# One integer addition of a bitwise weight conversion changes its engine, and a stretch of MLP work changes its place in the issue order

## The chip, the cores and the metric

The kernel runs on one core of a Trainium2 chip. Its time is the device time of one execution in microseconds; before the change it is 1355.24 us, the median of five runs (1354.21 to 1356.5). A profile of one execution goes with it. The engines that matter here are TensorE (PE, matrix products, with its weight loads shown as PEld), VectorE (DVE), ScalarE (ACT), GpSimd (POOL) and SyncE (SP, which here only issues transfers). Each engine works through its own instructions strictly in the order in which the program issues them, and waits for the others through semaphores; so the place of an instruction in its engine's order is as much a part of the kernel as the instruction itself.

## The reference, cut to what matters

```python
# q, k, v: 8 batches x 8 heads x 576 rows x 64; w_in 512 x 2048; w_out 2048 x 512
scores = scale * q @ k.T
thresh = max(scores, -1) - tau
scores = where(scores >= thresh, scores, -1e9)
attn = exp(scores - max) ; attn /= sum(attn) + 1e-9
x = (attn @ v)              # heads side by side: 4608 tokens x 512
h = x @ w_in
out = (0.5 * h * (1 + erf(h / sqrt(2)))) @ w_out
```

The weights w_in and w_out come as 64-bit floats. The chip has no arithmetic for them, so the kernel reads their two 32-bit halves and puts a 32-bit float together with shifts, masks and an integer addition.

## The kernel before, in words

**Slots.** The attention is cut into slots. A slot is one pair of heads and one chunk of 128 query rows (i = 0 to 3) or the 64 rows left over of both heads (i = 4). Slots 0 to 7 are chunks 0 and 1 of the first batch's four pairs, slots 8 to 19 their chunks 2, 3 and 4; from slot 20 on one pair after the other is taken with all five chunks. `BATCH` is 20, so n = 20 is the first slot of the second batch. Slots 0 to 19 are called early here; they turn matrices with TensorE (L339, L309), later slots with VectorE and transfers.

**A slot's instructions.** `scores` gives TensorE the product q k (L393) into one or two tiles of PSUM. The tag has two buffers, so the scores of slot n+1 can be written only when slot n has done with its own. `softmax_head` then issues, for each tile, the maximum of a row (L405, VectorE), the threshold (L406, GpSimd: a 128x1 instruction) and the exponential (L408, ScalarE). `softmax_tail` later issues the masking with the sum (L424, VectorE), which reads the scores, the threshold and the exponential, and frees the scores' buffer; in early slots GpSimd adds 1e-9 to the sum (L427), and VectorE inverts it in the next slot (L433). `weigh_v` multiplies with v (L527), and `divide_early` multiplies the result by the inverse on GpSimd (L454, 128x256).

**The weight conversion.** The weights are cut into 32 pieces of 128x512: 16 of w_in, then 16 of w_out. `load_piece` fetches a piece raw, both halves (L183, issued by GpSimd after the first four). The generator `conversions` issues for each piece: two ScalarE instructions, one that brings the high half to a power (L201, into a tile `power`) and one that writes the low half's bits straight into the weight tile (L202); then three on VectorE: a shift and mask (L209), an and/or with the sign (L211), and the integer addition of `power` to the low bits in the weight tile (L214). After L214 the next raw piece is fetched, and `converted[0]` counts the piece. Each VectorE step yields a nominal price (340, 720, 640). `convert` is a planner with a debt: it is given so many nanoseconds in each slot and takes steps until the debt is paid. In an early slot from the fourth on it is called twice: for at least one step (or 700 in chunk 4) ahead of `softmax_tail`, and at the end of the slot with 3100 (2000 in slots 1 and 2, without limit from slot 19 on).

**The MLP.** `fill` issues the work of the MLP block by block: 64 products of the first layer (L603), then 32 of the second (L618). How much is due in a slot comes from a curve of goals; the difference to the slot before is added to `owed`. A product is issued only if enough pieces are counted in `converted`. In early slots `fill` runs after the scores of the slot, later at the end of the slot. The first layer's results are held until slot 20, when ScalarE loads the Gelu table, runs Gelu on all of them (`gelus_held`, L576) and loads the Exp table again (L589). So the second layer of block 0 begins at the end of slot 20.

Of the kernel before, what the change touches and what calls it, by code (L numbers as in the profile page):

```python
# [9 lines left out]
U32 = mybir.dt.uint32  # L10
U8 = mybir.dt.uint8
AF = mybir.ActivationFunctionType
ALU = mybir.AluOpType
# [5 lines left out]
def kernel(  # L19
# [28 lines left out]
    nc = tc.nc  # L48
# [46 lines left out]
    op = late_end.enter_context(tc.tile_pool(name="op", bufs=2))  # L95
# [50 lines left out]
    for _ in range(3):  # L146
# [4 lines left out]
    pieces = [(w_in_sb[c][:, f:f + PIECE], moe_w_in[c * P:(c + 1) * P, f:f + PIECE])  # L151
              for f in range(0, d_ff, PIECE) for c in range(N_DM)]
# [3 lines left out]
    LATER = 2  # L156
    raws = []
    loaded = [0]
    converted = [0]
# [26 lines left out]
    def conversions():  # L186

        vec = nc.vector
        ahead = []
        while raws or ahead:
            if raws:
                dst, raw, slot = raws.pop(0)
                lo, hi = (raw.rearrange("p (f w) -> p f w", w=2)[:, :, i] for i in range(2))
                power = gp.tile([P, PIECE], U32, tag="g", name="power")  # L200
                nc.scalar.activation(power.bitcast(FP32), hi.bitcast(FP32), AF.Copy, bias=0.0, scale=2.0 ** -112)  # L201
                nc.scalar.activation(dst.bitcast(U32), lo, AF.Copy, bias=0.0, scale=2.0 ** -29)  # L202
                ahead.append((dst, hi, power, slot))
                yield 0
            if len(ahead) == LATER and converted[0] == len(pieces) - LATER:
                yield None
            if len(ahead) == 2 or not raws:
                dst, hi, power, slot = ahead.pop(0)
                vec.tensor_scalar(power, power, 3, 0x7FFFFFF8, op0=ALU.logical_shift_left, op1=ALU.bitwise_and)  # L209
                yield 340  # L210
                vec.scalar_tensor_tensor(power, hi, 0x80000000, power, op0=ALU.bitwise_and, op1=ALU.bitwise_or)  # L211
                x_free.extend(slot)
                yield 720
                vec.tensor_tensor(dst.bitcast(U32), power, dst.bitcast(U32), op=ALU.add)  # L214
                load_piece()
                converted[0] += 1
                yield 640

    conv = {"steps": None, "debt": 0.0}

    def convert(ns, least=0):

        if conv["steps"] is None:
            conv["steps"] = conversions()
        conv["debt"] += ns
        while conv["debt"] > 0 or least > 0:
            took = next(conv["steps"], None)
            if took is None:
                return
            conv["debt"] -= took  # L230
            least -= took
# [164 lines left out]
    def softmax_head(p, i):  # L396

        s = st[p]
        n = len(s["sc", i])
        nmx = small.tile([P, 2], FP32, tag="nmx", name="nmx")  # L400
        thr = s["thr", i] = small.tile([P, 2], FP32, tag="thr", name="thr")
        w = s["p", i] = work.tile([P, 2 * S], FP32, tag="p", name="p")
        for e in range(n):
            sc = s["sc", i][e][:, :, 0:HALF]
            nc.vector.tensor_reduce(nmx[:, e:e + 1], sc, axis=AXIS.XY, op=ALU.max, negate=True)  # L405
            nc.gpsimd.tensor_scalar(  # L406
                thr[:, e:e + 1], nmx[:, e:e + 1], -1.0, tau_eff, op0=ALU.mult, op1=ALU.subtract)
            nc.scalar.activation(  # L408
                w[:, e * S:(e + 1) * S].rearrange("p (h s) -> p h s", h=2), sc, AF.Exp, bias=nmx[:, e:e + 1], scale=1.0)
# [20 lines left out]
    def invert(p, i):  # L430

        den = st[p]["sum", i]
        nc.vector.reciprocal(den, den)  # L433
# [193 lines left out]
    def fill(ns, tokens):  # L627

        mlp["debt"] += ns
        while True:  # L630
            if mlp["next"] is None:
                n = mlp["n"]
                if n == PLAIN or (n + 1) * TOK > tokens:
                    break
                mlp["steps"] = block_steps(n)
                mlp["n"] += 1
                mlp["next"] = next(mlp["steps"])
            took, need = mlp["next"]
            if mlp["debt"] <= 0 or need > converted[0]:
                break  # L640
            mlp["debt"] -= took
            mlp["next"] = next(mlp["steps"], None)
# [22 lines left out]
    vec, pool = nc.vector, nc.gpsimd  # L665
# [15 lines left out]
    def weights_first():  # L681
        room = tail["room"] = early_end.enter_context(tc.tile_pool(name="wsum", bufs=1, side="right", reuse_waits="tile"))
        tail["s"] = room.tile([P, 4, 2, 2, P], FP32, name="s_out")
        tail["ss"] = room.tile([P, 4, 3, P], FP32, name="s_in")
        tail["sp"] = room.tile([P, 3, 4, P], FP32, name="s_plain")
        tail["t"] = room.tile([P, 4, 2, HD], FP32, name="t_out")
        w_in_sums(vec, 0)
# [338 lines left out]
    BATCH = HP * SLOTS  # L1026
# [18 lines left out]
    tokens = 0  # L1045
    owed = 0.0
# [3 lines left out]
    for n in range(len(slots) + WEIGH + 1):  # L1050
        p, i = slots[n] if n < len(slots) else divmod(n, SLOTS)
        early = p < EARLY
        last = slots[n - 1] if 0 < n <= len(slots) else None
        if p < NP:
            scores(p, i)
            softmax_head(p, i)
            if last and last[0] < EARLY:
                invert(*last)
            if p < HP - 1 and i == 0:
                turn_qk_early(p + 1)  # L1060
        elif n == len(slots):
            early_end.close()
            weights_first()
        gelus(0)
        if n == BATCH:
            gelus_held()
        table()
        for args in due:
            weigh_v(*args)
            divide_early(*args)  # L1070
        due = []
        if p > EARLY and i == WEIGH:
            for lo, hi in (0, WIDE), (WIDE, S):
                weigh_v(p - 1, lo, hi)
            if p == NP:
                divide(p - 1)
        owed += (goal(n) - goal(n - 1)) * BLK_NS * (PARTS[i] if not early and p < NP else 1.0)
        if early:
            fill(owed, tokens)
            owed = 0.0  # L1080
            table()
        if last and last[0] < EARLY and last[1] < NC:
            turn_p_early(*last)
        if early and n > 2:
            convert(0, 700 if i == NC else 1)
        if p < NP:
            softmax_tail(p, i)
        if p < NP and not early:
            turn_p(p, i)
        if p < NP and not early:  # L1090
            if i == 2:
                regroup(p, 1)
            if i > 2:
                regroup(p, i)
            if i == NC:
                divisors(p)
        if last and last[0] < EARLY and last[1] == NC:
            turn_p_early(*last)
        if p < 2 and i == 0:
            for _ in range(2):  # L1100
                load_piece()
            load_v_early(p + 2)
        if p == 1 and i == NC:
            load(HP)
        if n == BATCH - 3:
            load(HP + 1)
        if n == BATCH:
            for t in pd_tail + [turned_p[:, e, h, :, :] for e in range(2) for h in range(2)]:
                nc.gpsimd.memset(t[:, NB:4 * KR, :], 0.0)
        if EARLY < p < NP and i == DIVIDE:  # L1110
            divide(p - 1)
        if p >= HP and i == 1 and p + 2 < NP:
            loads = load_steps(p + 2)
        if p >= HP:
            next(loads, None)
        if p >= HP and i == 1 and p + 1 < NP or p == HP - 1 and i == 2:
            scale_q(p + 1)
        if p >= HP - 1 and i == 2 and p + 1 < NP:
            turn_qk(p + 1)
        convert(0 if n == 0 else 2000 if n < 3 else 3100 if n < BATCH - 1 else 1e9)  # L1120
        if not early:
            lag[0] = 2 if p < NP else 0
            fill(owed, tokens)
            owed = 0.0
        if last and last[0] < EARLY:
            if last[1] == 1:
                due.append((last[0], 0, TOK))
            if last[1] == NC:
                due.append((last[0], TOK, S))
        if n == START - 1:  # L1130
            tokens = TOK
        elif n == BATCH + 1:
            tokens = S
        elif p > EARLY and i == DIVIDE and p % HP == 0 or p == NP and i == WEIGH:
            tokens = p // HP * S
            leaving += [n for n in AWAY if n in x_blk and (n + 1) * TOK <= tokens]
        elif leaving and i < 2:
            put_away(leaving.pop(0))
# [35 lines left out]
```

## Time and profile before

| | value |
|---|---|
| median of five runs | 1355.24 us |
| the profiled execution itself | 1356.08 us, of it 1354.3 us span |
| slots 1 to 19, from the first L405 of slot 1 to that of slot 20 | 13.40 to 138.29 us |
| L209 shift and mask, VectorE | 32 of 419 ns (median) |
| L211 and/or, VectorE | 32 of 691 ns (median) |
| L214 integer addition, VectorE (shown as a custom instruction on 128x1024 uint16) | 32 of 692 ns (median) |
| VectorE busy over the span | 1056.8 us (78%) |
| GpSimd busy over the span | 623.5 us (46%) |
| largest idle of GpSimd | 366.8 us, ahead of L406, for the maximum L405 |

The page of a profile gives busy time by engine, forty equal slices of the span, and groups of instructions; the trace behind it can be asked for a table of stretches, for the instructions of one engine in order of time, or for one line. A row of the last kind reads: start, duration, engine, line, operation, output <- inputs, shape, number, and in brackets the idle time before it with what ended it. Where a duration includes waiting for a shared resource, the row is longer than its fellows. The start of one instruction to the start of the next (the pitch) can be shorter than the duration, since the recorded ends overlap a little.

A slot starts, for this document, with its first L405 in the VectorE rows: slot 2 at 19.57 us, slot 10 at 71.49, slot 16 at 110.85, slot 17 at 116.03, slot 18 at 125.88, slot 19 at 134.70, slot 20 at 138.29, slot 21 at 150.13, slot 22 at 159.19.

### The profile page before, as it was taken

Reading aid. Unit: us, or ns where it says so; the run is one execution under the profiler, and the core shown is the slowest. Engines: PE = TensorE matmul, PEld = TensorE weight load, DVE = VectorE, ACT = ScalarE, POOL = GpSimd, SP = SyncE. Lnnn points to the kernel's source line nnn. Section 1 sums busy time; section 2 is a strip of 40 time slices with the busy share of each in tenths; the row PEclk is TensorE's granted clock in tenths of the full one; section 3 lists DMA queues with packets and bytes.
Section 4 is the critical chain, followed back from the end, with each engine's and each line's share of the span. In section 5 each row is a group of like instructions: output and inputs, shape, how many; then the busy total and the mean of one; then the engine's idle time right before and its main releaser. Section 6 shows DMA issues by size and latency. Waiting matters only on the chain.

```text
span 1354.3 us, 19808 instructions
## 1 busy us (share of the span) xinstructions
PE 1323.9 (98%) x6282; PEld 892.5 (66%) x6282; DVE 1056.8 (78%) x2029; ACT 605.6 (45%) x1027; POOL 623.5 (46%) x1065
## 2 busy tenths in 40 slices
PE   8799899999999999999999999999999999999998
PEld 6476457467457457557557557568787787877877
DVE  6987677788888888878888888875758598385775
ACT  7786527547547538527637636413201112211120
POOL 5442354555555554554555552145363513625530
PEclk9799899999999999999999999999999999999999
DMA  8642277677778787787688777500000041000003
GB/s 271 178 158 50 58 158 162 142 162 185 155 178 184 161 192 179 161 206 170 152 202 188 151 174 157 120 9 1 0 1 0 8 117 32 1 1 0 1 0 78
DMA packets 209782, 152.40 MB, mean 113 GB/s; under 512 B 113360, under 2 KB 193088, under 8 KB 209680
## 3 DMA queue, kind: packets, MB, share of 16 engines
q1 hardware_dynamic: 188224, 112.53, 37.5%
q0 software_dynamic: 21024, 38.32, 9.9%
q8 instruction: 51, 0.84, 0.3%
q14 instruction: 51, 0.42, 0.1%
q10 hardware_dynamic: 432, 0.30, 0.1%
HBM read 55.97 MB, written 12.52 MB: 51 GB/s over the span
## 4 chain that ended last, share of the span: by engine, by line
PE 88%; DMA 1%; ACT 1%; DVE 1%; issue 0%; SPq 0%; POOL 0%; DVEq 0%; ACTq 0%; POOLq 0%
PE bank L791 34%; PE o_ps L618 17%; PE hT L603 15%; PE sc L393 12%; PE xT L527 10%; DMA x<-xall 1%; ACT p L408 0%; DVE nmx L405 0%; PE tr L339 0%; DVE p L424 0%; ACT L576 0%; SPq L476 0%; SPq L474 0%; ACT g L570 0%; ACT xall L537 0%
## 5 line engine op out<-in xcount | busy, mean ns | idle before, releaser
L408 ACT ACTIVATE p<-sc,nmx 128x576 f32<-128x576 f32 x288 | 201.9, 738 | 287.1 <-DVE nmx L405 286.9
L424 DVE SCALAR_TENSOR_TENSOR p<-sc,thr,p 128x576 f32<-128x576 f32 x288 | 225.2, 815 | 66.7 <-ACT p L408 64.1
L406 POOL TENSOR_SCALAR thr<-nmx,tau_eff 128x1 f32<-128x1 f32 x288 | 89.7, 312 | 383.3 <-DVE nmx L405 366.8
L603 PE MATMUL hT<-xall,w_in 128*128 128x256 f32 x1024 | 242.8, 386 | 2.6 <-ACT g L570 2.6
L405 DVE TENSOR_REDUCE nmx<-sc 128x1 f32<-128x576 f32 x288 | 205.3, 750 | 51.1 <-PE sc L393 50.0
L618 PE MATMUL o_ps<-w_out,g 128*128 128x512 f32 x512 | 239.4, 608 | 3.7 <-ACT g L576 3.7
L603 PEld LDWEIGHTS hT<-xall,w_in 128*128 128x128 f32 x1024 | 189.6, 190 | 53.1 <-issue 23.0
L673 DVE TENSOR_TENSOR c<-c,bank 128x320 f32<-128x320 f32 x304 | 147.2, 487 | 33.7 <-PE bank L791 20.1
L673 DVE TENSOR_TENSOR o<-o,bank 128x256 f32<-128x256 f32 x240 | 99.6, 419 | 93.8 <-PE bank L791 88.8
L618 PEld LDWEIGHTS o_ps<-w_out,g 128*128 128x128 f32 x512 | 94.0, 192 | 114.4 <-issue 107.8
L393 PE MATMUL sc<-kT,qT 64*128 64x288 f32 x960 | 162.2, 434 | 7.0 <-DVE p L424 6.3
L527 PE MATMUL xT<-pT,v 128*64 128x256 f32 (+1 forms) x1280 | 167.2, 415 | 0.1
L488 DVE STREAM_TRANSPOSE turned_p<-p 128x1152 f32<-128x1152 f32 x112 | 154.4, 1379 | 3.9
L393 PEld LDWEIGHTS sc<-kT,qT 64*128 64x128 f32 x960 | 92.5, 188 | 81.5 <-issue 68.0
L527 PEld LDWEIGHTS xT<-pT,v 128*64 128x64 f32 x1280 | 90.5, 140 | 75.5 <-issue 17.4
L791 PE MATMUL bank<-w_out,c 128*128 128x256 f32 x480 | 120.2, 381 | 0.5 <-DVE o L673 0.5
L259 POOL DMA_DIRECT2D v<-in_v_dram x208 | 110.9, 536 | 4.0 <-issue 1.8
L791 PEld LDWEIGHTS bank<-w_out,c 128*128 128x128 f32 x480 | 89.9, 190 | 18.8 <-DVE o L673 3.0
L844 ACT ACTIVATE c<-c 128x320 f32<-128x320 f32 (+1 forms) x80 | 46.9, 624 | 114.6 <-DVE c L673 114.5
L791 PE MATMUL bank<-t_out,c 128*128 128x256 f32 x320 | 82.8, 381 | 0.0
L791 PE MATMUL bank<-t_out,g 128*128 128x256 f32 x320 | 82.1, 379 | 0.0
L673 POOL TENSOR_TENSOR c<-c,g 128x320 f32<-128x320 f32 (+1 forms) x40 | 50.5, 1271 | 67.5 <-DVE c L673 67.5
(179 smaller groups left out, 1743.8 us busy)
## 6 DMA issues: line engine op xcount, KB each, us to landing
pT<-turned_p SPq DMA_DIRECT2D x448, 160.0 KB, 3.6
pT<-pd_tail SPq DMA_DIRECT2D x112, 80.0 KB, 3.0
q<-in_q_dram POOLq DMA_DIRECT2D x104, 72.0 KB, 3.7
k<-in_k_dram POOLq DMA_DIRECT2D x104, 72.0 KB, 3.2
inv<-turned SPq DMA_DIRECT2D x54, 128.0 KB, 4.1
v<-in_v_dram POOLq DMA_DIRECT2D x156, 40.0 KB, 3.1
out_dram<-o SPq DMA_DIRECT2D x40, 128.0 KB, 2.4
xall<-in_moe_w_out_dram POOLq DMA_DIRECT2D x9, 512.0 KB, 4.0
```

The source lines that it names most:

```text
L259: eng.dma_start(t[r:P:4, e, 0:n, :], rows[:, r * KR:r * KR + n, :])
L393: nc.tensor.matmul(sc[e][:, h, 0:HALF], lhsT=lhsT, rhs=s["kT"][rows, at:at + HALF], start=True, stop=True)
L405: nc.vector.tensor_reduce(nmx[:, e:e + 1], sc, axis=AXIS.XY, op=ALU.max, negate=True)
L406: nc.gpsimd.tensor_scalar(thr[:, e:e + 1], nmx[:, e:e + 1], -1.0, tau_eff, op0=ALU.mult, op1=ALU.subtract)
L408: nc.scalar.activation(w[:, e * S:(e + 1) * S].rearrange("p (h s) -> p h s", h=2), sc, AF.Exp, bias=nmx[:, e:e + 1], scale=1.0)
L424: nc.vector.scalar_tensor_tensor(row, sc[e][:, :, 0:HALF], thr[:, e:e + 1], row, op0=ALU.is_ge, op1=ALU.mult, accum_out=den[e])
L488: nc.vector.transpose(turned_p[:, :, i // 2, 0:NB, i % 2 * Q:(i % 2 + 1) * Q], w.rearrange("p (e b i) -> p e b i", e=2, i=Q))
L527: nc.tensor.matmul(to, lhsT=s["v"][:, e, c, :], rhs=rhs, start=(c == 0), stop=(c == KR - 1))
L603: nc.tensor.matmul(hT[:, j % 2, :], lhsT=w_in_sb[c][:, j * P:(j + 1) * P], rhs=x_blk[n][:, c, :], start=(c == 0), stop=(c == N_DM - 1))
L618: nc.tensor.matmul(o[:, 0:d_model], lhsT=g[j][:, m * P:(m + 1) * P], rhs=w_out_sb[j], start=(j == 0), stop=(j == N_DF - 1))
L673: eng.tensor_tensor(out, a, b, op=ALU.add)
L791: nc.tensor.matmul(to, lhsT=l, rhs=r, start=start and k == 0, stop=k == len(pairs) - 1, skip_group_check=not start)
```

## The change

```diff
         ahead = []
+        done = 0
         while raws or ahead:
...
-            if len(ahead) == LATER and converted[0] == len(pieces) - LATER:
+            if len(ahead) == LATER and done == len(pieces) - LATER:
                 yield None
...
                 x_free.extend(slot)
                 yield 720
-                vec.tensor_tensor(dst.bitcast(U32), power, dst.bitcast(U32), op=ALU.add)
+                sums_due.append((dst.bitcast(U32), power))
                 load_piece()
-                converted[0] += 1
-                yield 640
+                done += 1
+                yield 0
+
+    sums_due = []
+
+    def add_low_bits():
+
+        while sums_due:
+            dst, power = sums_due.pop(0)
+            nc.gpsimd.tensor_tensor(dst, power, dst, op=ALU.add)
+            converted[0] += 1
...
             scores(p, i)
             softmax_head(p, i)
+            add_low_bits()
...
-        convert(0 if n == 0 else 2000 if n < 3 else 3100 if n < BATCH - 1 else 1e9)
+        convert(0 if n == 0 else 1200 if n < 3 else 2200 if n < BATCH - 1 else 1e9)
         if not early:
             lag[0] = 2 if p < NP else 0
-            fill(owed, tokens)
-            owed = 0.0
+            if n != BATCH:
+                fill(owed, tokens)
+                owed = 0.0
```

The third VectorE instruction of each piece is no longer issued. Its operands are put on a list, and the additions on the list are issued to GpSimd in the next slot, behind that slot's thresholds; only then is the piece counted. The next raw piece is fetched without the addition being waited for. A piece now costs 1060 in the planner's money, and a slot's budget falls from 3100 to 2200 (2000 to 1200 in slots 1 and 2). In slot 20 `fill` isn't called; what was due there stays in `owed` and is issued at the end of slot 21, behind the scores of slot 21.

## The prediction

> **What bounds the kernel now.** I read the page first, for the engine that is full, then the slots one by one.
>
> ```profile
> PE 1323.9 (98%) x6282; PEld 892.5 (66%) x6282; DVE 1056.8 (78%) x2029; ACT 605.6 (45%) x1027; POOL 623.5 (46%) x1065
> ...
> PE   8799899999999999999999999999999999999998
> ...
> DVE  6987677788888888878888888875758598385775
> ...
> PEclk9799899999999999999999999999999999999999
> ```
>
> TensorE is full from the sixth slice (170 us) on; only the first five have gaps, and there its clock falls too. The change touches only those slices. Since TensorE is full after them, a microsecond won or lost before 160 us should reach the end whole. The table of stretches, cut at the slots (here 6, 7, 12, 17, 18, 20), shows who is full there:
>
> ```profile
> core 0: us, PE busy (x) PEld busy (x) DVE busy (x) ACT busy (x) POOL busy (x), PEclk, DMA share, GB/s
> ...
> 44.62:51.04 6.42, 3.73 (x12) 2.34 (x14) 6.21 (x14) 4.77 (x9) 2.46 (x6) 0.67 0.52 158
> 51.04:58.32 7.28, 7.13 (x52) 4.67 (x48) 5.62 (x14) 5.09 (x11) 2.91 (x6) 0.82 0.48 143
> ...
> 82.99:91.30 8.31, 8.02 (x53) 6.50 (x50) 6.04 (x14) 5.56 (x13) 3.70 (x7) 1.00 0.42 151
> ...
> 116.03:125.88 9.85, 9.85 (x65) 7.01 (x63) 8.06 (x18) 5.89 (x12) 1.29 (x4) 1.00 0.12 30
> 125.88:134.70 8.82, 6.20 (x25) 5.00 (x25) 6.32 (x13) 5.07 (x11) 2.60 (x5) 0.81 0.01 3
> ...
> 138.29:150.13 11.84, 8.09 (x26) 3.72 (x27) 5.53 (x12) 8.91 (x14) 1.34 (x8) 0.86 0.01 1
> ```
>
> The column after the length is TensorE, the third VectorE, the fifth GpSimd. Slot 6 is VectorE's: 6.21 of 6.42 us. Slots 7 and 12, with a product with v, aren't: there L209 waits for ScalarE's L201 (1.59 and 2.20 us idle), and ScalarE for TensorE. GpSimd has room: 2.5 to 3.7 us a slot.
>
> **What the removal is worth.** In slot 6 the conversion's starts on VectorE stand like this:
>
> ```profile
> 47.82 0.69 DVE L211 SCALAR_TENSOR_TENSOR power<-xall,power 128x512 uint32<-128x512 uint32 x1
> 48.54 0.69 DVE L214 CUSTOM_DVE_ANT_0 w_in<-power,w_in 128x1024 uint16<-128x1024 uint16 x1
> 49.15 0.42 DVE L209 TENSOR_SCALAR power<-power 128x512 uint32<-128x512 uint32 x1
> ```
>
> From start to start L211 costs 0.72 to 0.73 us, L214 0.61, and L209 0.45: 1.79 a piece before, 1.18 after. The 32 pieces save 32 x 0.61 = 19.5 us of VectorE, if nothing takes its place. I follow the planner's debt by hand: 3100/1700 = 1.82 pieces a slot before, 2200/1060 = 2.08 after. So slots 3 to 15 hold 24 L209, 23 L211 and 24 L214 before (42.2 us) and 27, 27 and none after (31.9 us): 10.3 us less. The conversion also ends earlier: slot 18 has its last two pieces before, slot 17 after; slot 18 then holds none.
>
> **What the addition costs on GpSimd.** No row shows an integer addition there. The nearest are float additions and subtractions of the same shape, and L454:
>
> ```profile
> L673 POOL TENSOR_TENSOR s_out<-w_in 128x512 f32<-128x512 f32 x6 | 7.6, 1266 | 0.0
> ...
> L454 POOL TENSOR_TENSOR xall<-xall,inv 128x256 f32<-128x256 f32 x8 | 6.8, 848 | 13.8 <-ACT inv L448 13.8
> ```
>
> I take 1.27 us, the row of the same shape and operation. Bounds: 0.69 us, as on VectorE, and 2.5 us, twice the row. The Trainium skill speaks against the move: "GPSIMD Engine Reference", section 4.1, keeps elementwise work on VectorE, and section 3.1 gives 4497 ns for 2048 floats, by which I estimate 1.12 us for 512; the sum below would then be about 1.4 us lower (nine blocks of 0.15 us). The float rows here say 1.27.
>
> The cost isn't GpSimd's time but what it takes from VectorE. In slot 5, L211 meets an L454:
>
> ```profile
> 40.21 0.81 DVE L424 SCALAR_TENSOR_TENSOR p<-sc,thr,p 128x576 f32<-128x576 f32 x1
> ...
> 40.95 1.05 DVE L211 SCALAR_TENSOR_TENSOR power<-xall,power 128x512 uint32<-128x512 uint32 x1
> ```
>
> ```profile
> 39.03 0.45 POOL L406 TENSOR_SCALAR thr<-nmx,tau_eff 128x1 f32<-128x1 f32 x1 [0.27 <-DVE den L433]
> 40.71 0.75 POOL L454 TENSOR_TENSOR xall<-xall,inv 128x256 f32<-128x256 f32 x1 [1.22 <-ACT inv L448]
> ```
>
> L211 takes 1.05 us instead of 0.69 and ends 0.6 after L454 does: it stood still while GpSimd ran. The other stretched L211 (1.20 and 1.11 us, at 129.43 and 106.86) stand beside an L454 as well. In the other direction L406, 0.29 us alone, takes 0.45 to 0.72 beside an L209 or L211. L424 isn't touched (0.81 us beside GpSimd's L551 at 195 us).
>
> So in a full slot that starts at T: second threshold done at about T+2.0, first addition to T+3.3, under the two L424 (to T+3.3): free. The second runs to T+4.6 and meets the L209 and L211 after L424, which wait: about 1.2 us. If VectorE gets in first, the addition gets in at the next gap, and the price is the same. **Sum, slots 3 to 15:**
> - Slots bound by VectorE (3, 4, 5, 6, 8, 10, 11, 13, 14): instructions +0.24 - 0.77 - 1.22 x 6 - 0.77 = -8.6 us; blocks 1.2 in seven of them, 2.4 in slot 13 (three additions), none in slot 3 (one): +10.8 us. Net +2.2.
> - Slots 7, 9, 12, 15 wait for ScalarE; the removed L214 stood in that wait, so nothing is won. In 9 and 12 one L211 or L209 more follows the wait: +0.6 and +0.5.
> - Slots 1 and 2: one L214 less ahead of L405 of slot 2: -0.6. Slot 3 starts when TensorE's scores are there: 0.
>
> Together +2.7 us, by bounds from -8.1 (no block) to +14 (an addition of 2.5 us blocks once for 2.5).
>
> **Slots 16 to 19.** Here TensorE shows what VectorE delays:
>
> ```profile
> 128.60 1.94 PE L603 MATMUL hT<-xall,w_in 128*128 128x256 f32 x4 [2.62 <-ACT g L570]
> ...
> 142.95 5.98 PE L618 MATMUL o_ps<-w_out,g 128*128 128x512 f32 x10 [3.75 <-ACT g L576]
> ```
>
> L570 stands behind the exponential of slot 18, that behind L405 at 125.88, and that behind slot 17's conversion (122.76 to 125.88). After the change slot 16 has one L211 left, so slot 17 can start with its scores (114.7 instead of 116.0), does three steps ahead of L424, waits for q's scaling as now, and has one L211 behind its transposes: L405 of slot 18 at about 123.0, the four L603 at 125.8 to 126.4, 2.2 to 2.8 us earlier. What is late next is TensorE's own queue. The 2.62 us gap goes, and with it the slow products behind it (4 L603 in 1.94 and 9 L339 in 2.14 us, against 0.92 and 1.15 at full clock): up to 2 us more. I take -4.3; from -2.0 to -5.5.
>
> **The moved MLP work.** Ten L618 leave slot 20 and stand behind the scores of slot 21 and the product with v there; twenty follow. Now TensorE is idle for 3.75 us at 139.2, then runs L618, and the scores of slot 21 start at 148.86. After: scores at 141.5 (buffers free after L424), L527 at 144.1 (after L359), L618 from about 147.5 to 148.7, 20 x 0.45 = 9.0 us, scores of slot 22 at 156.6 to 157.7 instead of 157.91. Gelu is done at 146.5 and holds nothing up. The exponential of slot 21 still waits for the table (147.85), with time to spare. -0.8 us, from 0 to -1.4. No transfer is moved by this; SP's queue gets block 0's two output stores about a microsecond earlier.
>
> GpSimd's own queue: the raw fetches, L427 and L454 stand behind the additions. Two thresholds 0.8, additions 2.5, waits for VectorE 0.6, L427 0.5, two fetches 1.25: 5.7 us, 6.5 with L454, in a slot of 6.3 to 7.3. It just fits; raw pieces are fetched eight ahead and land in 4 to 8 us, so later fetches cost nothing.
>
> **Sum:** 2.7 - 4.3 - 0.8 = -2.4 us against the profiled 1356.08 us. That run is 0.84 above the median; on the median it gives 1352.8 us. A difference under 0.2% (2.7 us) is what a measurement here can't tell from none.
>
> **The rivals.** *No blocking* (0.20): the additions fall into GpSimd's 366.8 us of waiting and VectorE hardly sees them, for instance because they are shorter. Then the early slots shrink: -8.1 - 4.3 - 0.8 = -13, about 1342 us; half blocking gives 1347. For it: GpSimd idles; against it: L211's 1.05 us.
> *GpSimd becomes the bound* (0.27), the slower side. If an addition takes more than about 1.4 us, or waits more for VectorE, the 5.7 to 6.5 us reach the slot's length; the next threshold is late, then L424, then the scores. From there each 0.1 us costs 0.2 a slot, 13 slots, 2.6 us: at 1.65 us +6 on the forecast, 1359; at 2.5 us about 1375. For it: no row for integers; against it: floats at 1.27.
> *Nothing gained* (0.10): TensorE and ScalarE set slots 16 to 19 too, and the early slots come out even: 1355.
> The forecast has 0.43: 1350 to 1356.
>
> **Chances.** Faster by over 0.2%: 0.20 + 0.43 x 0.44 = 0.39. Slower: 0.27 + 0.43 x 0.07 = 0.30. Within: 0.31. The range leaves out the far ends of both rivals: 1345 to 1361.
>
> **What would show it.** Right: L211 or L209 of 1.5 to 1.9 us beside an addition of about 1.27, one in most slots from 4 to 14; slot 10 starting at 71 to 74 us; no idle before L603 near 126; L618 in one run of twenty. Wrong: additions without stretched VectorE rows (no blocking), or L424 waiting for L406 (GpSimd bound).

## The result and the profile after

The kernel after the change takes 1352.79 us (median of 24 runs, 1350.03 to 1355.79), beside 1355.3 us for the kernel before in the same comparison (43 runs). The ratio is 0.9981, with a 95% interval of 0.9975 to 0.9986: a gain of 2.5 us (1.9 to 3.4), real but small. The profiled execution took 1352.03 us, of it 1349.9 us span. In the new kernel the old line L209 is L210, L211 is L212, and everything from L214 on stands ten lines further down (maximum L415, threshold L416, masking L434, first MLP layer L613, second L628); ScalarE's two conversions are L202 and L203; the new addition on GpSimd is L226. In the kernels of the experiments some lines stand one or two off from these.

The page of after, total busy time and slices:

```profile
PE 1322.4 (98%) x6282; PEld 893.8 (66%) x6282; DVE 1047.7 (78%) x1997; ACT 605.0 (45%) x1027; POOL 659.0 (49%) x1097
...
DVE  6887677788888888888888888874758698385775
```

VectorE has 32 instructions less but is only 9.1 us less busy, where 32 additions of 0.69 us would be 22; rows of other instructions that got longer, shown below, make up most of the rest. GpSimd has 32 more and is 35.5 us busier. The new group, asked for by its line:

```profile
L226 POOL TENSOR_TENSOR w_in<-power,w_in x16: 1258/1264/1696, 20.9 to 75.9; 128x512 uint32<-128x512 uint32 x16
L226 POOL TENSOR_TENSOR w_out<-power,w_out x16: 1253/1266/1730, 80.0 to 128.9; 128x512 uint32<-128x512 uint32 x16
```

The integer addition takes 1.26 us, the length of the float row. The table of stretches of after, in the columns known from before, with the same slots (6, 7, 12, 17, 18, 20):

```profile
45.17:51.13 5.96, 3.27 (x10) 2.10 (x12) 5.93 (x12) 4.77 (x9) 5.31 (x9) 0.72 0.64 188
51.13:59.15 8.02, 7.79 (x54) 5.02 (x50) 6.09 (x12) 5.16 (x11) 5.48 (x9) 0.78 0.46 159
84.02:93.21 9.19, 8.90 (x59) 7.15 (x56) 6.36 (x14) 5.98 (x13) 6.19 (x10) 1.00 0.53 177
118.19:125.92 7.73, 6.61 (x35) 4.72 (x37) 7.65 (x15) 3.95 (x9) 2.99 (x5) 1.00 0.03 7
125.92:133.66 7.74, 7.45 (x54) 5.70 (x49) 3.05 (x8) 3.88 (x9) 4.25 (x7) 1.00 0.14 35
138.40:144.18 5.78, 3.30 (x16) 2.13 (x18) 5.53 (x13) 4.96 (x8) 1.34 (x8) 0.93 0.00 0
```

Slot 6, bound by VectorE, became 0.46 us shorter; slots 7 and 12 became 0.74 and 0.88 us longer; slots 17 and 18 shorter by 2.12 and 1.08. Slot 20 has lost its ten L628, which slot 21 now runs. The next two fences show one full slot, VectorE's rows of after and then GpSimd's:

```profile
46.90 0.81 DVE L434 SCALAR_TENSOR_TENSOR p<-sc,thr,p 128x576 f32<-128x576 f32 x1
...
47.63 0.81 DVE L434 SCALAR_TENSOR_TENSOR p<-sc,thr,p 128x576 f32<-128x576 f32 x1
...
48.37 1.78 DVE L212 SCALAR_TENSOR_TENSOR power<-turned_p,power 128x512 uint32<-128x512 uint32 x1
50.07 0.41 DVE L210 TENSOR_SCALAR power<-power 128x512 uint32<-128x512 uint32 x1
50.52 0.69 DVE L212 SCALAR_TENSOR_TENSOR power<-xall,power 128x512 uint32<-128x512 uint32 x1
```

```profile
46.68 0.45 POOL L416 TENSOR_SCALAR thr<-nmx,tau_eff 128x1 f32<-128x1 f32 x1 [0.26 <-DVE den L443]
47.10 2.50 POOL L226 TENSOR_TENSOR w_in<-power,w_in 128x512 uint32<-128x512 uint32 x2
```

The two additions run from 47.10 to 49.60. The two L434 (46.90 to 48.44) run beside them at their usual 0.81 us, but the L212 that starts at 48.37 needs 1.78 us instead of 0.69 and ends only after the second addition. TensorE's rows of after show the other two steps, no idle ahead of L613 near 126 to 128, and one run of twenty L628:

```profile
128.29 2.86 PE L613 MATMUL hT<-xall,w_in 128*128 128x256 f32 x12
...
148.60 8.85 PE L628 MATMUL o_ps<-w_out,g 128*128 128x512 f32 x20
157.38 1.24 PE L403 MATMUL sc<-kT,qT 64*128 64x288 f32 x8
```

**Where the time went.** Profiles begin up to 1.3 us apart (slot 0 starts at 8.6 to 9.9 us), so the lengths between slot starts are compared:

| us | slots 0 to 2 | 3 to 15 | 16 to 19 | 20 to 24 | sum | median, difference from before |
|---|---|---|---|---|---|---|
| before | 16.30 | 85.31 | 27.44 | 36.34 | 165.39 | |
| after | 14.81 | 89.34 | 24.68 | 34.77 | 163.60 (-1.8) | -2.5 |

Slots 3 to 15 lose 4.0 us, the rest wins 5.8. After slot 24 the two traces run in step until about 594 us. From there the shift grows by 3 us, at two places near 600 and 700 us where ScalarE's copy waits for a store. A second profile of after (`a_again`) had -1.7 us up to slot 24 and only -1.1 behind 594 us, so that second part is mostly chance. Of the median's 2.5 us, about 1.8 stand in the slots that the change touches; the remaining 0.7 were not found in one place.

### The profile page after: what moved, and what is told of

Its sections match the earlier page's. It is cut to its first block, busy times and chain, and to the rows that moved or that the text cites. A ratio compares the mean times of both kernels' runs of the same rounds, so it can differ in the third digit from the quotient of the medians.

```text
span 1349.9 us, 19821 instructions
## 1 busy us (share of the span) xinstructions
PE 1322.4 (98%) x6282; PEld 893.8 (66%) x6282; DVE 1047.7 (78%) x1997; ACT 605.0 (45%) x1027; POOL 659.0 (49%) x1097
## 4 chain that ended last, share of the span: by engine, by line
PE 93%; DVE 3%; ACT 2%; issue 1%; DMA 0%; POOL 0%; DVEq 0%; SPq 0%; ACTq 0%; POOLq 0%
PE bank L801 34%; PE o_ps L628 17%; PE hT L613 16%; PE sc L403 14%; PE xT L537 12%; DVE nmx L415 1%; ACT p L418 1%; DVE p L434 1%; PE tr L349 1%; ACT pT L356 1%; DMA x<-xall 0%; DVE power L212 0%; ACT power L202 0%; DVE power L210 0%; PE tr L456 0%
## 5 line engine op out<-in xcount | busy, mean ns | idle before, releaser
L434 DVE SCALAR_TENSOR_TENSOR p<-sc,thr,p 128x576 f32<-128x576 f32 x288 | 225.2, 815 | 68.9 <-ACT p L418 67.0
L416 POOL TENSOR_SCALAR thr<-nmx,tau_eff 128x1 f32<-128x1 f32 x288 | 88.0, 307 | 366.9 <-DVE nmx L415 354.6
L415 DVE TENSOR_REDUCE nmx<-sc 128x1 f32<-128x576 f32 x288 | 205.3, 749 | 53.6 <-PE sc L403 52.4
L613 PE MATMUL hT<-xall,w_in 128*128 128x256 f32 x1024 | 241.8, 385 | 0.0
L628 PE MATMUL o_ps<-w_out,g 128*128 128x512 f32 x512 | 236.8, 603 | 0.0
L613 PEld LDWEIGHTS hT<-xall,w_in 128*128 128x128 f32 x1024 | 189.4, 190 | 50.0 <-issue 23.0
L628 PEld LDWEIGHTS o_ps<-w_out,g 128*128 128x128 f32 x512 | 93.1, 190 | 109.1 <-issue 106.8
```

The costliest lines, as they stand in the source:

```text
L416: nc.gpsimd.tensor_scalar(thr[:, e:e + 1], nmx[:, e:e + 1], -1.0, tau_eff, op0=ALU.mult, op1=ALU.subtract)
L434: nc.vector.scalar_tensor_tensor(row, sc[e][:, :, 0:HALF], thr[:, e:e + 1], row, op0=ALU.is_ge, op1=ALU.mult, accum_out=den[e])
L613: nc.tensor.matmul(hT[:, j % 2, :], lhsT=w_in_sb[c][:, j * P:(j + 1) * P], rhs=x_blk[n][:, c, :], start=(c == 0), stop=(c == N_DM - 1))
L628: nc.tensor.matmul(o[:, 0:d_model], lhsT=g[j][:, m * P:(m + 1) * P], rhs=w_out_sb[j], start=(j == 0), stop=(j == N_DF - 1))
```

## The experiments

Lengths between slot starts, as above, from one profile each; the last two columns are the added-up excess of L210 and L212 rows that are over 0.3 us too long (against 0.42 and 0.69), and VectorE's waits for ScalarE's conversion, both in slots 3 to 15. A median's difference is from the median of the runs of before that were made together with it (1354.8 to 1355.8 us):

| kernel | 0-2 | 3-15 | 16-19 | 20-24 | sum | median, difference | stretched | waits for ScalarE |
|---|---|---|---|---|---|---|---|---|
| before | 16.30 | 85.31 | 27.44 | 36.34 | 0 | 0 | 1.2 | 6.3 |
| e1_only_mlp | 16.33 | 85.21 | 27.42 | 35.34 | -1.1 | -0.9 | 1.2 | 6.2 |
| e6_before_fast | 16.21 | 88.24 | 23.55 | 36.68 | -0.7 | -0.6 | 1.4 | 3.2 |
| after | 14.81 | 89.34 | 24.68 | 34.77 | -1.8 | -2.5 | 13.4 | 10.9 |
| e2_only_add | 14.80 | 88.37 | 24.68 | 36.65 | -0.9 | -1.2 | 13.4 | 10.1 |
| e3_no_add | 14.78 | 86.71 | 23.60 | 35.37 | -4.9 | -5.9 | 0 | 19.0 |
| e4_ahead | 14.80 | 92.70 | 23.59 | 34.18 | -0.1 | -1.0 | 6.3 | 17.6 |
| e8_no_rush | 14.81 | 88.98 | 23.94 | 34.20 | -3.5 | -3.7 | 13.5 | 10.6 |
| e9_twice | 14.80 | 109.50 | 29.81 | 34.20 | +22.9 | +21.2 | 21.9 | 8.6 |
| e11_pace_between | 14.80 | 85.05 | 25.13 | 34.54 | -5.9 | -6.4 | 9.7 | 10.9 |
| e5_old_pace | 14.81 | 81.02 | 25.47 | 34.59 | -9.5 | -7.8 | 10.2 | 6.4 |
| e10_no_add_old_pace | 14.78 | 81.29 | 25.45 | 34.84 | -9.0 | -10.2 | 0.4 | 11.9 |
| e12_pace_1800 | 14.77 | 82.99 | 24.91 | 35.02 | -7.7 | -6.8 | 8.3 | 9.8 |

The sums agree with the medians within 2 us; they come from one execution each, so the columns show where time goes and the medians how much. Up to slot 15 the kernels after, `e2_only_add` and `e8_no_rush` issue the same instructions, and yet slots 3 to 15 take 89.34 (89.47 in the second profile), 88.37 and 88.98 us. Most of that stands in slot 7, which takes 8.02, 8.11, 7.33 and 7.72 us at a granted TensorE clock (the column PEclk of the table of stretches, 1.00 is full speed) of 0.78, 0.77, 0.85 and 0.80. A difference of one microsecond in that column is within this scatter.

**The change again, for its scatter** (`a_again`). Expected:

> The kernel after once more, for a second profile. The theory: from slot 0 to slot 25 it gains 1.8 us against before, as in the first profile, and what the first profile gained behind 570 us (2.9 us, at the wait of the copy L547 for the store of an x block) is chance and will differ by a microsecond or two. The rival: the change moves those waits, and they are shorter again by 2 to 3 us.

Measured: 1354.41 us in a single run, 14.80, 89.47, 24.68 and 34.79 us in the four columns. The gain up to slot 24 repeats within 0.15 us, as expected; behind 594 us it is 1.1 us instead of about 3.

**One half at a time.** `e1_only_mlp` is before with only the moved MLP work, `e2_only_add` is after without it.

```diff
-            fill(owed, tokens)
-            owed = 0.0
+            if n != BATCH:
+                fill(owed, tokens)
+                owed = 0.0
```

> The kernel before with only the second half of the change: slot 20 issues no MLP work, slot 21 issues twenty L618 behind its scores; the addition stays on VectorE. The theory: it is worth 0.6 us by itself (0.64 between the starts of slots 20 and 22 in the profiles of before and after), so 1354.7; slots 1 to 20 as before. The rival, that the moved work gives the whole 2.5 us and the move of the addition nothing, expects 1352.8.

> The kernel after with slot 20's MLP work put back into slot 20: only the addition is moved, with the new budgets. The theory: slot 16 starts 2 to 3 us later than before, slot 20 level with before or up to 1 us earlier, the end 1 to 2 us earlier: 1353.4 to 1354.2. The rival (the moved work gives everything): 1355.3.

Measured: 1354.45 us (ratio 0.9993, 0.9984 to 1.0001) and 1354.07 us (0.9997, 0.9988 to 1.0006). Both are within 0.3 us of what the theory had, but neither half alone can be told from none. The differences of the medians, -0.9 and -1.2, add up to about the whole. In the traces the move shortens slots 20 to 24 by 1.0 us (e1 against before), and the conversion half wins 0.9 us in all, which is within the scatter named above.

**The addition left out** (`e3_no_add`). The third step of the conversion isn't done at all, the pace is that of after; what is left out is the addition of `power` to the low bits.

```diff
             dst, power = sums_due.pop(0)
-            nc.gpsimd.tensor_tensor(dst, power, dst, op=ALU.add)
             converted[0] += 1
```

> The kernel after without the addition on any engine: it leaves the third step of the conversion out, so the weights are incomplete and only the time is read. The theory (an addition on GpSimd beyond the first in a slot stops VectorE's next L212 for its length): no L212 over 0.8 us but beside an L464; slot 16 starts 7 to 10 us earlier than after's 113.72, and the time is 1342 to 1346. The rival (TensorE and ScalarE set the early slots, and the additions cost nothing): 1352 to 1353, slot 16 as after. A second rival (GpSimd's queue is late): the thresholds, not the L212, move earlier, with the same total as the theory.

Measured: 1349.42 us (0.9961, 0.995 to 0.9973). VectorE's rows of e3 in slots 6 and 7:

```profile
46.43 0.68 DVE L212 SCALAR_TENSOR_TENSOR power<-turned_p,power 128x512 uint32<-128x512 uint32 x1
...
51.49 0.69 DVE L212 SCALAR_TENSOR_TENSOR power<-turned_p,power 128x512 uint32<-128x512 uint32 x1
56.03 0.51 DVE L210 TENSOR_SCALAR power<-power 128x512 uint32<-128x512 uint32 x1 [3.85 <-ACT power L202]
```

No L212 is stretched any more, so the standing still is the additions' doing. But slots 3 to 15 are 1.4 us *longer* than before, without any addition anywhere, and both numbers that were expected (1342 to 1346, and 1352 to 1353) are missed. The bracket of the last row says why: VectorE gets done sooner and then waits 3.85 us for ScalarE's L202. In slots 3 to 15 these waits are 19.0 us instead of 10.9 in after, and VectorE's idle time in all is 23.1 instead of 12.8: of 13.4 us of stretched rows, about 10 come back as waiting.

ScalarE isn't the end of that chain. Its rows of e3 in slots 7 and 12, and in the second fence the table of stretches for the same two slots:

```profile
53.16 0.39 ACT L546 COPY xall<-xT 128x256 f32<-128x256 f32 x1 [2.67 <-PE xT L536]
...
87.60 1.07 ACT L355 COPY pT<-tr 128x512 f32<-128x512 f32 x2 [3.22 <-PE tr L348]
```

```profile
48.22:57.19 8.97, 8.74 (x56) 5.31 (x54) 5.08 (x13) 5.80 (x13) 2.88 (x7) 0.75 0.42 127
80.69:90.97 10.28, 9.99 (x67) 7.74 (x64) 5.44 (x13) 6.88 (x15) 3.82 (x8) 1.00 0.50 169
```

The copies, behind which the conversions stand, wait for TensorE, and TensorE is full there: in slots 7, 9, 12 and 15 together it is busy 36.7 of 37.2 us in e3, 32.8 of 33.3 in after and 29.9 of 30.4 before. A shorter slot ahead only leaves it more to do in these: in slots 11 and 12 TensorE's rows count 37 and 53 instructions before, 31 and 59 in after, 24 and 67 in e3. So without the additions slots 5, 6, 8, 10, 11, 13 and 14 are 6.6 us shorter than in after, and slots 7, 9, 12 and 15 are 3.9 us longer. Slots 6 and 7 together take 13.98 us in after and 13.96 in e3, slots 11 and 12 15.14 in both (the first pair varies with the clock, 13.29 us in e2; the second doesn't).

**The block avoided by order** (`e4_ahead`). The newest addition goes ahead of the thresholds, the others stay behind them.

```diff
+                sums_due.append((dst.bitcast(U32), power))
                 yield 720
-                sums_due.append((dst.bitcast(U32), power))
...
             scores(p, i)
+            add_low_bits(True)
             softmax_head(p, i)
             add_low_bits()
```

The lines that let `add_low_bits(True)` issue the newest addition alone are left out here.

> The kernel after with one of a slot's two additions issued ahead of the slot's thresholds instead of behind them: that of the piece whose L212 ends the slot before. It should run beside L415 (scores in PSUM), the other beside L434, and neither meet a step of the conversion. The theory: L212 at 0.69 us in most slots, thresholds 0.3 to 0.6 us later but in time for L434; slot 16 starts 4 to 9 us earlier than after, 1345 to 1349 us. The rival (GpSimd's queue is late): the thresholds' delay reaches L434 and the time is 1353 to 1358.

Measured: 1354.33 us (0.9998, 0.999 to 1.0007). VectorE's rows of e4:

```profile
48.17 0.69 DVE L212 SCALAR_TENSOR_TENSOR power<-turned_p,power 128x512 uint32<-128x512 uint32 x1
...
57.80 0.52 DVE L210 TENSOR_SCALAR power<-power 128x512 uint32<-128x512 uint32 x1 [3.68 <-ACT power L202]
...
94.58 3.38 DVE L212 SCALAR_TENSOR_TENSOR power<-turned_p,power 128x512 uint32<-128x512 uint32 x1
```

In slots 6 to 9 the block goes (L212 at 0.69 us; over slots 3 to 15 the stretched rows add up to 6.3 us instead of 13.4), and the same thing happens as in e3: the wait for ScalarE takes its place. On top, VectorE's L436 (the masking in this kernel) waits eight times in slots 3 to 15, 3.0 us in all, for a threshold that now stands behind an addition; in after it never does there. The time is in the rival's range. But of the 6.0 us by which slots 3 to 15 are longer than in e3, 4.9 stand in slots 13 and 14, and there the block hasn't gone: the L212 of the last row stands still through both additions, the scores of slot 14 come late, and TensorE then runs twelve products of the first layer in 5.17 us, at a granted clock of 0.68 over the slot (2.75 us for twelve at 1.00 in slot 15 of after).

**The pace** (`e5_old_pace`, `e6_before_fast`). The budget of a slot changes with nothing else: after with 1930 instead of 2200 (1930/1060 = 1.82 pieces a slot, as before), and before with 3530 instead of 3100 (2.08 pieces, as after).

```diff
-        convert(0 if n == 0 else 1200 if n < 3 else 2200 if n < BATCH - 1 else 1e9)
+        convert(0 if n == 0 else 1200 if n < 3 else 1930 if n < BATCH - 1 else 1e9)
```

> The kernel after with a budget of 1930 instead of 2200 in slots 3 to 18: 1.82 pieces a slot, the pace of before, with the addition on GpSimd. The theory now (the early slots go at the pace of ScalarE's conversion work, 1.27 us a piece, and not of VectorE's): slots 3 to 16 get shorter than after's by up to 3.8 us (three pieces fewer), slots 17 to 19 longer by about as much, the time 1352 to 1354.5. The rival (VectorE's steps and their blocks set the early slots): the same pieces still cost 1.79 us each, the end slots keep their gain less the two later pieces, 1350 to 1352.

> The kernel before with a budget of 3530 instead of 3100: 2.08 pieces a slot, the pace of after, with the addition left on VectorE. If the gain of slots 17 to 19 comes from the conversion ending earlier, and not from the engine of the addition, it shows here too: slot 18 level or earlier against slot 16, but slot 16 itself 4 to 5 us later, the time 1354 to 1357. The rival (the earlier end is the whole gain, whatever the engine): 1352.5 to 1353.5.

Measured: e5 1347.76 us (0.9948, 0.9933 to 0.9963), faster than both kernels and below both of its expected ranges; e6 1354.95 us (0.9999, 0.999 to 1.0008), in the expected range. So at the old pace the move of the addition, with the MLP work, is worth 7.8 us, and the faster pace that came with it gives back 5.0; at the faster pace (e6 to after) the same move is worth about 2. The gain of the end slots does come from the conversion's earlier end and not from the engine: e6, with the addition on VectorE, takes 23.55 us in slots 16 to 19, less than after, and pays for it with 2.9 us in slots 3 to 15. Slot 4 shows how. VectorE's row of after there, and in the second fence the one of e6, which has the addition on VectorE:

```profile
37.54 0.43 DVE L210 TENSOR_SCALAR power<-power 128x512 uint32<-128x512 uint32 x1 [1.25 <-ACT power L202]
```

```profile
38.76 0.43 DVE L209 TENSOR_SCALAR power<-power 128x512 uint32<-128x512 uint32 x1 [0.88 <-ACT power L201]
```

Both wait for ScalarE's conversion of a piece, and both stand ahead of the next slot's maximum. ScalarE's rows of after, then those of e5, and last VectorE's rows of e5:

```profile
36.83 0.68 ACT L202 ACTIVATE power<-xall 128x512 f32<-128x512 f32 x1
37.41 0.69 ACT L203 ACTIVATE w_in<-xall 128x512 uint32<-128x512 uint32 x1
37.99 0.71 ACT L202 ACTIVATE power<-turned_p 128x512 f32<-128x512 f32 x1
38.57 0.69 ACT L203 ACTIVATE w_in<-turned_p 128x512 uint32<-128x512 uint32 x1
39.40 0.74 ACT L418 ACTIVATE p<-sc,nmx 128x576 f32<-128x576 f32 x1
```

```profile
35.78 0.68 ACT L202 ACTIVATE power<-xall 128x512 f32<-128x512 f32 x1
36.36 0.67 ACT L203 ACTIVATE w_in<-xall 128x512 uint32<-128x512 uint32 x1
36.93 1.37 ACT L418 ACTIVATE p<-sc,nmx 128x576 f32<-128x576 f32 x2
```

```profile
35.47 1.42 DVE L415 TENSOR_REDUCE nmx<-sc 128x1 f32<-128x576 f32 x2
...
36.87 0.41 DVE L210 TENSOR_SCALAR power<-power 128x512 uint32<-128x512 uint32 x1
```

ScalarE comes to the conversion of that piece late in both, behind the copies of turned matrices. In after VectorE's L210 and L212 of the piece still belong to slot 4, and the maximum of slot 5 has to wait for them until 38.61 us; in e5 the maximum goes first and L210 follows in slot 5. Slot 4 takes 7.29 us in after, e3 and e6 alike, with the addition on GpSimd, nowhere and on VectorE, and 5.62, 5.24 and 5.96 us in e5, e10 and before. Here the place of the steps, which the pace moves, sets the length, and the addition doesn't.

**The addition left out at the old pace** (`e10_no_add_old_pace`: e3's edit and e5's together; the addition is left out) and **a pace between** (`e11_pace_between`: 2060, or 1.94 pieces a slot).

> The kernel with the budget 1930 and without the addition on any engine: it leaves the third step of the conversion out, so the weights are incomplete and only the time is read. Against the run with 1930 and the additions (1347.8) it gives the price of the blocks at a pace at which ScalarE isn't full. The theory: 3 to 7 us below it, 1341 to 1345. The rival (the additions cost nothing, ScalarE alone sets the pace): 1346.5 to 1348.

> The kernel after with a budget of 2060 instead of 2200 (1.94 pieces a slot). The theory (each further piece in an early slot costs its ScalarE time there): between 1347.8 and 1352.8, about 1350, slot 16 between 104.6 and 113.7. The rival (it is only a matter of which step falls where in a slot): outside these, or no difference to one of the two.

Measured: e10 1345.66 us (0.9927, 0.9912 to 0.9942), e11 1349.46 us (0.9953, 0.9937 to 0.997). At the old pace the additions cost 2.1 us by the medians, less than the 3 to 7 expected, with intervals that overlap, and nothing in the traces (slots 3 to 15 take 81.02 us with them and 81.29 without): when the additions go, VectorE's stretched rows lose 9.9 us and its idle time grows by 8.1 (10.2 to 18.3), of it 5.4 for ScalarE's conversion. e11 is where it was expected: the medians fall from 2.08 over 1.94 to 1.82 pieces a slot, the last step with intervals that overlap.

**A slower pace still** (`e12_pace_1800`: 1800, or 1.70 pieces a slot).

> The kernel after the change with a budget of 1800 a slot instead of 2200: 1800/1060 = 1.70 pieces a slot, still slower than before's 1.82. Budgets of 2200, 2060 and 1930 gave 1352.8, 1349.5 and 1347.8 us. Theory A: the time falls with a lower pace only as long as the pieces left over still fit beside the work of slots 16 to 18; at 1.70 some four more pieces than at 2.08 stand behind slot 15, slot 19's budget is without limit and takes what is left in one stretch, and VectorE's conversion again stands ahead of the maxima of slots 18 to 20. Then slot 16 starts earlier than at 1930 (104.6 us) but slot 20 later (130.1), and the time is 1347 to 1351 us. Theory B: ScalarE's and VectorE's conversion work costs the early slots more than the late ones whatever the pace; then slot 20 starts earlier than 130 us too and the time is under 1347 us.

Measured: 1348.0 us (0.9942, 0.9928 to 0.9955), not to be told from e5. That is in theory A's range, but not for its reason: slots 3 to 15 aren't shorter than in e5 but 2.0 us longer (82.99 us; slot 16 starts at 106.81 us instead of 104.64), though fewer pieces fall there. Slot 4 takes 7.30 us again, because at this pace too an L210 stands ahead of the next maximum and waits there, 2.01 us, for ScalarE's L202. So in slot 4 it isn't the pace as such that costs time, but which steps it puts ahead of the next maximum; for the whole column that isn't shown. Whether the time rises again at a still slower pace isn't shown.

**The rush at the end** (`e8_no_rush`): once the last two pieces must wait for the others to be counted, the debt is cleared instead of running on, so that slot 17 doesn't take three steps ahead of its masking.

```diff
             if took is None:
+                conv["debt"] = 0.0
                 return
```

> The kernel after, but the planner's debt is set to zero when the conversion pauses ahead of its last two pieces: slot 17 then takes one step (L210) ahead of L434 instead of three, and the other three behind the transposes. The theory (slot 17's L434 is 2 us late because three steps and an addition stand ahead of it, and the scores of slot 18 wait for it): slot 18 starts about 1 us earlier, the time is 0.5 to 1.5 us below after's, 1351.3 to 1352.3. The rival (the steps behind the transposes delay L415 of slot 18 by as much): no change, 1352.8.

Measured: 1351.88 us (0.9975, 0.9966 to 0.9984), 0.9 below after, with intervals that overlap. In the trace slots 16 to 19 win 0.7 us, but not where that was expected: the masking of slot 17 comes 1.73 us after the slot's start instead of 3.88, and still slot 18 starts 0.6 us later against slot 17, because the steps behind the transposes hold up its maximum, as the rival says. The gain stands in slot 18 (6.35 us instead of 7.74).

**GpSimd overloaded** (`e9_twice`): a second addition of the same operands behind each, into `power`, which nobody reads any more.

```diff
             nc.gpsimd.tensor_tensor(dst, power, dst, op=ALU.add)
+            nc.gpsimd.tensor_tensor(power, power, dst, op=ALU.add)
```

> The kernel after with a second addition of the same shape behind each one on GpSimd (its result goes into the tile power, which nobody reads again). It stands for an addition of 2.5 us. The prediction's rival, GpSimd as the bound, priced this at about 1375: the next slot's L416 is late, then L434. The theory agrees on the mechanism: L434 waits for L416 by 1 to 3 us in most of slots 4 to 16; 1365 to 1378. If GpSimd still hides it, 1353 to 1358.

Measured: 1377.01 us (1.0158, 1.0138 to 1.0178). VectorE's rows of e9:

```profile
48.89 0.17 DVE L444 RECIPROCAL den<-den 128x2 f32<-128x2 f32 x1 [1.40 <-POOL den L438]
...
49.91 0.82 DVE L435 SCALAR_TENSOR_TENSOR p<-sc,thr,p 128x576 f32<-128x576 f32 x1 [0.54 <-POOL thr L417]
```

VectorE now waits for what stands behind the additions on GpSimd: in slots 3 to 15 10.2 us for the sums' 1e-9 (L438) and 3.7 us, seven times, for the next threshold (L417). The time was expected, but of its path only the smaller part: the inversion (L444) waits more than the masking. In after neither of the two ever waits for GpSimd in these slots; this bound is real, and the change stays short of it.

## Why the prediction came out, step by step

The forecast was 1352.8 us, the measured median is 1352.79. The agreement of the sum is better than its terms deserve: the interval of the gain is 1.9 to 3.4 us, and inside the first term three errors cancel.

- **Slots 1 to 15, predicted +2.7 us.** Measured +2.5 from slot 0 to slot 16. That is luck. The nine slots called "bound by VectorE" cost 1.1 us instead of 2.2; slots 7, 9, 12 and 15 cost 2.9 instead of 1.1; slots 1 and 2 win 1.5 instead of 0.6, since slot 2 itself got 0.7 us shorter and the sum had it at 0. The wrong step is to price the slots one by one. VectorE's instructions were counted right, but in slots 7, 9, 12 and 15 TensorE is full, and what the slot ahead of them wins or loses on VectorE largely turns up there with the other sign. Against before, the nine slots of e3, without any addition, win 5.45 us and the four lose 6.85; the additions then cost the nine 6.6 us and give the four 3.9 back.
- **The pace in that term.** It entered only as seven VectorE instructions more (three L210, four L212). That 2.08 instead of 1.82 pieces also move steps ahead of a maximum, where they wait for ScalarE, was left out: slot 4 alone is 1.3 us longer than before, with or without the addition. In slots 3 to 15 the addition's removal at the old pace wins 4.0 us (e10), the faster pace then costs 5.4 (e10 to e3) and the blocks at that pace 2.6 (e3 to after): -4.0 + 5.4 + 2.6 = +4.0. Taken in the other order the blocks cost nothing (e10 to e5, -0.3) and the pace 8.3 (e5 to after). The two are not separate costs, and a sum that adds them can't show that.
- **An addition of 1.27 us, not 0.69 or 2.5.** Measured 1.26.
- **The mechanism of the block.** Shown: L210 or L212 of 1.4 to 1.8 us beside the second addition in most slots, L434 at 0.81 us beside the first, no stretched row in e3. Its price per block was right (0.9 to 1.1 us longer against 1.2); its effect on the end was not. One reading on the way was off: the L406 of 0.72 us stands beside an L214 (at 104.34 us), not beside an L209 or L211, of which the longest is 0.68.
- **Slots 16 to 19, predicted -4.3 us (-2.0 to -5.5).** Measured -2.8. The idle before the first layer's products is gone as foreseen. At the start of slot 19 the gain over slot 16 stands at 3.9 us; then the scores of slot 20 wait for TensorE's own queue (VectorE is idle for 2.27 us there) and 1.1 us are given back. In slot 17 an L210 of 1.49 us ahead of the masking, a block that I had not placed there, costs some of it: e8, without these steps ahead, is 0.7 us shorter in slots 16 to 19, though the gain stands in slot 18. So the chain was right, and the last part of the term, up to 2 us for faster products, was too large.
- **The moved MLP work, predicted -0.8 us.** Measured -1.0 (e1). The times were right within 0.7 us: scores of slot 21 at 141.0 (141.5), its product with v at 143.5 (144.1), twenty L628 from 148.6 (147.5 to 148.7) in 8.85 us (9.0), scores of slot 22 at 157.4 (156.6 to 157.7). How much the move gives differs with the granted clock, which the prediction left out here: the product with v takes 4.66 us in after, with a granted clock of 0.50 in the first two microseconds of slot 21, and slots 20 and 21 are 0.6 us shorter than before; in e8 it takes 2.88 us at 1.00, and they are 2.2 us shorter.
- **The rivals.** *No blocking* was priced at 1342 us. Even with the addition left out, e3 takes 1349.4 and e10 1345.7: the price was too large for the same reason as the first term, since most of what the blocks cost VectorE comes back as waiting. *GpSimd becomes the bound* was priced at about 1375 us for an addition of 2.5 us; two additions a piece (e9) gave 1377. By the prediction's own rule (2.6 us for each 0.1 us over 1.4) the price would have been about 1381 and not 1375. It is the right mechanism at about the right place, and it decides only if the addition is much longer than it is.
- **Left open.** That VectorE waits for ScalarE, and ScalarE for TensorE, is shown by the rows; that the conversions are late because of the copies ahead of them is read from the order of the rows, and no instruction of ScalarE or TensorE was taken away to try it. About 0.7 us of the gain have no place.

## What to carry to other kernels

When an instruction leaves a busy engine, ask at once who is next, in that stage and in the one behind it: remove the instruction altogether in a trial and see how much of its time comes back as a wait for another engine. That shows what moving it can win at most while all else stays as it is. When a change also alters a budget or a pace, try each at the other's setting; here the move was worth 7.8 us at the old pace and about 2 at the new, and e5, which only moves the addition, beats e3, which removes it but keeps the new pace. And a sum that agrees with the clock is no proof of its terms: compare them stage by stage.

## What the runs showed of the hardware

- A VectorE instruction on two operands in SBUF (L212), or L210 on one, stood still for 0.9 to 1.1 us, nearly the whole of the second GpSimd addition, and finished after it; the masking (L434), which reads the scores from PSUM, ran at 0.81 us beside the first. When VectorE gets in first the addition is the one that is longer, up to 1.73 us instead of 1.26. Beside two additions that were issued around one 128x1 threshold (e4), an L212 stood still through both and took 3.38 us.
- 32-bit integer addition and float addition of 128x512 take the same time on GpSimd (1.26 and 1.27 us).
- In slot 23 some L628 run at 0.45 us each and others at 0.55 to 0.58: the granted clock over that stretch is 1.00 in after, 0.82 in before and 0.77 in e12. This moves the sums of the tables by 0.9 us and follows none of the edits: e5 has the short form, e3 and e12 the long one. In slot 21 the same goes for the product with v: 4.66 us in after and 2.88 in e8, with a granted clock of 0.50 and 1.00 in the slot's first two microseconds.
- The wait for one and the same store differs by 2 us between two executions. From the chain of before, and then of after:

```profile
596.70 8.56 DMA x<-xall
```

```profile
595.38 6.50 DMA x<-xall
```

Such a wait can make a pair of single profiles differ by more than a change of this size does.
